# Forgetting attention with a spectral mix: a load moved ahead of a blocked one, mode products moved to mid-step, a small load moved to another queue

## The chip, the cores and the metric

The kernel runs on one core of a Trainium2 chip. The metric is the time of one execution on the device, in microseconds (us). The profile's span is some 1.7 to 2.0 us shorter than that time, so spans are compared with spans and times with times.

## The reference

There are two stages. The first is causal attention with a decay made from a forget gate f: for 8 batches and 8 heads, 576 positions, head width 64. The second takes the result x (8 x 576 x 512), keeps the 64 lowest frequencies of a real Fourier transform along the positions, multiplies each with its own complex 512 x 512 matrix, transforms back, and finishes with one more product.

```python
log_f = np.log(np.clip(f, 0.0001, 1.0)); cum = np.cumsum(log_f, axis=-1)
scores = scale * q @ k.T + cum[:, :, :, None] - cum[:, :, None, :]      # causal, softmax
x = attn @ v                                                           # (B, S, H*D)
X = np.fft.rfft(x, axis=1);  Xr, Xi = X.real[:, :64], X.imag[:, :64]
Yr = einsum('bmd,mde->bme', Xr, w_r) - einsum('bmd,mde->bme', Xi, w_i)
Yi = einsum('bmd,mde->bme', Xr, w_i) + einsum('bmd,mde->bme', Xi, w_r)
u = x + np.fft.irfft(Y, n=576, axis=1)
out = u + np.maximum(u @ w_ch, 0.0)
```

w_r and w_i are 64 x 512 x 512 in float32 each: together 134 MB, most of what the kernel reads.

## The kernel before

The kernel does both stages at once. There are 32 steps, one per head and pair of batches (and one more for the pipeline's end), and two steps share one *pair* of heads, whose q, k and v come in one load each. While these steps compute the attention, weight tiles of 2 x 512 KB (in bf16; the source is float32) stream in through a ring of 9 slots. `emit_modes(n)` multiplies with tile n and so frees its slot; `next_w()` issues the next tile, which needs a free slot. All loads that change the type come from one engine, POOL, and keep their program order. So a load that waits for a slot holds up every load behind it.

```python
NRING = 9                                  # weight tiles in the ring
STG = 3                                    # staged pairs of q, k, v

def pool_dma(dst, src):
    tc.keep_in_program_order(nc.gpsimd.dma_start(dst, src))

def emit_loads(pr):                        # k, q, v of one pair
    ...
        if nm == "v" and pr < 2:
            nc.sync.dma_start(dst, ap)     # the first two v: no cast, Sync queue
        else:
            pool_dma(dst, ap)
...
nc.sync.dma_start(ft[:], f.rearrange("b h s -> (b h) s"))
emit_loads(0)
... # log, cumulative sum, transposes, exp: the decay factors, then the Fourier basis
for s in range(NS + 1):                    # NS = 32 steps, B = 8, NTH = 32
    pr, h = s // 2, s % 2
    if h == 0 and pr + STG - 1 < NPR:
        emit_loads(pr + STG - 1)
    if s < 10 and nload < min(NRING, 3 + 3 * s // 4):
        next_w()                           # fill the ring
    if s == 10:
        pool_dma(wch[:], moe_w_ch.rearrange("(eb p) e -> p eb e", p=128))
    ... # transposes of the next pair, scores 0, first attention-value group, scores 1 and 2
    if s >= 1:
        emit_av(s - 1, [3, 4])             # second attention-value group
    ... # scores 3, v back, Fourier products of a finished pair
    if s > B:
        while nmode < (s - B) * NTH // (NS - B):
            emit_modes(nmode)              # first one: step 9; frees a ring slot
            nmode += 1
            next_w()                       # tenth tile: first one that needs a freed slot
```

The softmax here doesn't subtract the row's maximum and nothing guards it: scores larger than these inputs give would overflow.

## Time and profile before

| | before |
|---|---|
| time, median of the first 3 runs | 448.64 us |
| span of the profiled run | 446.5 us |
| bytes read from HBM | 163.73 MB |
| last weight landed | 405.3 us |
| rest (late products, output) | 41.2 us |

These are lines of the profile's page for the kernel before: the DMA rows of the 40-slice view (11.16 us a slice; first the mean busy share of the 16 DMA engines in tenths, then what they moved), the HBM total, and the chain of waits that ended last, by engine.

```profile
DMA  8999999999999999999999999999999999991698
GB/s 203 206 233 233 234 234 233 152 233 206 233 234 207 234 216 224 233 211 229 231 210 235 211 212 211 211 211 211 211 211 211 211 211 211 211 196 28 225 362 296
HBM read 163.73 MB, written 9.44 MB: 388 GB/s over the span
DMA 58%; PE 18%; DVE 7%; ACT 7%; issue 3%; POOL 1%; SPq 1%; DVEq 0%; ACTq 0%; POOLq 0%
```

From the first slice to 400 us the DMA engines are busy. The GB/s row counts what is written, in bf16 for most loads, so the reads behind 211 GB/s are about twice that. The one odd value is 152, in the eighth slice (78 to 89 us). A closer look, in windows of 1 us of the kernel before; the last two columns are the DMA share (1.2 is a full stream here) and GB/s:

```profile
core 0: us, PE busy (x) PEld busy (x) DVE busy (x) ACT busy (x) POOL busy (x), PEclk, DMA share, GB/s
78.00:79.00 1.00, 1.00 (x20) 0.83 (x21) 1.00 (x4) 0.64 (x3) 0.00 (x0) 1.00 1.24 207
79.00:80.00 1.00, 0.90 (x29) 0.88 (x30) 0.90 (x4) 0.99 (x2) 0.00 (x0) 1.00 0.78 129
80.00:81.00 1.00, 1.00 (x35) 0.97 (x31) 0.73 (x2) 0.04 (x1) 0.07 (x1) 1.00 0.28 51
81.00:82.00 1.00, 1.00 (x17) 0.65 (x15) 1.00 (x3) 1.00 (x2) 0.96 (x2) 1.00 0.11 27
82.00:83.00 1.00, 1.00 (x18) 0.76 (x17) 1.00 (x2) 1.00 (x2) 1.00 (x2) 1.00 0.63 48
83.00:84.00 1.00, 1.00 (x18) 0.55 (x18) 1.00 (x3) 0.77 (x2) 0.85 (x2) 1.00 1.18 179
```

For some 4 us the stream breaks. Who is late? This is the timeline of POOL, the issuer, at that time (start, duration, engine, line, what; in brackets the idle time before it and what ended it), and of the tensor engine's mode products (PE, L138):

```profile
64.76 0.74 POOL L88 DMA_DIRECT2D wb<-in_moe_w_i_dram  x1 [1.75 <-DMA wb<-in_moe_w_r_dram]
80.93 0.74 POOL L88 DMA_DIRECT2D wb<-in_moe_w_r_dram  x1 [15.43 <-PE tp L437]
...
82.43 0.71 POOL L88 DMA_DIRECT2D stk<-in_k_dram  x1
...
84.85 0.77 POOL L88 DMA_DIRECT2D wch<-in_moe_w_ch_dram  x1
```

```profile
77.70 0.17 PE L138 MATMUL A<-XT,wb 128*128 128x16 bf16 x1 [0.52 <-DVE XT L581]
79.70 0.92 PE L138 MATMUL A<-XT,wb 128*128 128x16 bf16 x31
```

The ninth tile was issued at 64.76 us. Then POOL stands still for 15.43 us, until the first mode product (32 matmuls, of which 31 run at 79.70 to 80.62) frees a slot. The profile names a neighbouring tensor-engine group as the releaser, but the tile it waits to overwrite is the one that L138 reads. Behind the blocked tile stand the next pair's k, q and v and w_ch, though none of them needs that slot. What had been issued before runs out at 79.4 us.

A load is spread over 16 DMA engines and counts as landed when all 16 have reported. The trace records each of the 16 reports. Here are those of the last loads around the hole (first and last report of each, worked out from the trace, in us):

```
                            first    last     spread
last load before the hole   79.42    81.45    2.03
first load after it         85.56    86.03    0.47
last weight of all          400.16   405.30   5.14
```

A 512 KB weight half takes 2.54 us at the stream's pace. So the first report lost 85.56 - 79.42 - 2.54 = 3.60 us in the hole, and the last one lost 86.03 - 81.45 - 2.54 = 2.04 us. I call these *first-engine loss* and *last-engine loss*, though the trace doesn't say which of the 16 engines a report comes from. The hole also pulls the spread together here, from 2.03 to 0.47 us: nearly all start even after it.

At the start, f is issued on Sync ahead of v. The timelines of Sync and Activation in the kernel before:

```profile
0.81 0.59 SPq L238 DMA_DIRECT2D Yacc<-in_f_dram  x1
1.46 1.07 SPq L217 DMA_DIRECT2D stv<-in_v_dram  x2
```

```profile
0.80 1.28 ACT L285 ACT_TABLE_LOAD   x1 [0.80 <-PEq L873]
3.66 0.68 ACT L285 ACTIVATE Yacc<-Yacc 64x576 f32<-64x576 f32 x1 [1.58 <-DMA Yacc<-in_f_dram]
```

f lands at 3.64 us, and the logarithm at 3.66 starts the chain that leads to the decay factors, and so to every step.

### The profile page before, as it was taken

How to read it: one execution, taken by the hardware profiler on the slowest of the kernel's cores; microseconds unless marked ns; L12 is line 12 of the kernel's file. 1: busy time of each engine (PE TensorE's matmuls, PEld its weight loads, DVE VectorE, ACT ScalarE, POOL GpSimd, SP SyncE). 2: the span in 40 equal slices, each digit the busy share in tenths (PEclk: the TensorE clock that was granted, in tenths of full speed). 3: DMA queues.
4: the chain of work that ended last, by engine and by line, in shares of the span. 5: the costliest groups of instructions: out<-in, count | busy, mean ns of one | idle time of the engine just before them, and what ended most of it. 6: DMA issues, size and time to landing. Idle time of an engine off the chain costs nothing.

```text
span 446.5 us, 11102 instructions
## 1 busy us (share of the span) xinstructions
PE 327.1 (73%) x4791; PEld 222.6 (50%) x4791; DVE 237.3 (53%) x602; ACT 202.4 (45%) x296; POOL 146.1 (33%) x194
## 2 busy tenths in 40 slices
PE   2388888989788788768597969999822238527993
PEld 1255555766566566556465746656612224323441
DVE  5768888776676546656377664223300002103894
ACT  3378888647567454664446533443200002102442
POOL 7333330534343323323333223232322323200661
PEclk9999999959599555897769578999955558856998
DMA  8999999999999999999999999999999999991698
GB/s 203 206 233 233 234 234 233 152 233 206 233 234 207 234 216 224 233 211 229 231 210 235 211 212 211 211 211 211 211 211 211 211 211 211 211 196 28 225 362 296
DMA packets 66431, 97.25 MB, mean 218 GB/s; under 512 B 3376, under 2 KB 44848, under 8 KB 66384
## 3 DMA queue, kind: packets, MB, share of 16 engines
q0 software_dynamic: 62480, 85.34, 103.3%
q1 hardware_dynamic: 3824, 11.09, 6.9%
q8 instruction: 37, 0.61, 0.5%
q10 hardware_dynamic: 80, 0.13, 0.1%
q14 instruction: 10, 0.08, 0.0%
HBM read 163.73 MB, written 9.44 MB: 388 GB/s over the span
## 4 chain that ended last, share of the span: by engine, by line
DMA 58%; PE 18%; DVE 7%; ACT 7%; issue 3%; POOL 1%; SPq 1%; DVEq 0%; ACTq 0%; POOLq 0%
DMA wb<-in_moe_w_i_dram 30%; DMA stk<-in_k_dram 13%; DMA stq<-in_q_dram 11%; ACT E L496 4%; DMA wb<-in_moe_w_r_dram 3%; PE tp L437 3%; PE pav L534 3%; PE pxw L680 3%; PE ps L489 3%; PE A L138 2%; DVE XT L581 2%; PE vp L461 1%; DVE uo L821 1%; PE ptr L669 1%; ACT KT L450 1%
## 5 line engine op out<-in xcount | busy, mean ns | idle before, releaser
L496 ACT ACTIVATE E<-ps 128x1024 bf16<-128x1024 f32 (+1 forms) x128 | 104.5, 859 | 39.3 <-PE ps L489 27.2
L138 PE MATMUL A<-XT,wb 128*128 128x16 bf16 x2048 | 71.6, 172 | 56.8 <-DMA wb<-in_moe_w_i_dram 35.0
L138 PEld LDWEIGHTS <-wb 128*128 128x128 bf16 x2048 | 64.0, 100 | 72.6 <-DMA wb<-in_moe_w_i_dram 38.2
L88 POOL DMA_DIRECT2D wb<-in_moe_w_r_dram x65 | 47.5, 731 | 134.7 <-PE A L138 30.4
L88 POOL DMA_DIRECT2D wb<-in_moe_w_i_dram x65 | 47.1, 725 | 78.2 <-DMA wb<-in_moe_w_i_dram 45.1
L489 PE MATMUL ps<-QTs,KT 64*128 64x64 bf16 (+4 forms) x384 | 57.5, 319 | 6.1 <-ACT E L496 5.9
L534 PE MATMUL pav<-va,E 128*128 128x65 bf16 (+1 forms) x1088 | 55.9, 210 | 4.3 <-DVE x_all L556 2.6
L534 PEld LDWEIGHTS <-E 128*128 128x128 bf16 (+1 forms) x1088 | 45.1, 114 | 15.8 <-issue 5.6
L153 DVE TENSOR_TENSOR YT<-A,Yacc 128x128 bf16<-128x128 f32 x24 | 8.9, 369 | 77.2 <-PE A L138 77.2
L511 DVE TENSOR_TENSOR E<-E,trimask 128x256 bf16<-128x256 bf16 (+2 forms) x128 | 38.2, 317 | 6.8 <-ACT E L496 6.4
L450 ACT COPY KT<-tp 128x640 bf16<-128x640 bf16 (+1 forms) x32 | 22.1, 745 | 26.6 <-PE tp L437 26.4
L687 ACT CAST XW<-pxw 128x512 bf16<-128x512 f32 x36 | 20.3, 587 | 29.8 <-PE pxw L680 25.1
L680 PE MATMUL pxw<-wch,yy 128*128 128x512 bf16 x144 | 33.5, 382 | 0.0
L699 ACT CAST yy<-pyw 128x512 bf16<-128x512 f32 x8 | 4.7, 586 | 60.7 <-PE pyw L692 60.7
L437 PE MATMUL tp<-ident_bf,kb 128*128 128x128 bf16 x144 | 16.1, 269 | 19.1 <-DVE kb L421 19.1
L556 DVE TENSOR_TENSOR x_all<-pav,rcp 128x384 bf16<-128x384 f32 x64 | 29.2, 456 | 0.9
L454 ACT COPY VT<-tp 128x640 bf16<-128x640 bf16 (+1 forms) x32 | 22.5, 753 | 12.6 <-PE tp L437 12.4
L489 PEld LDWEIGHTS <-KT 64*128 64x128 bf16 x384 | 18.1, 98 | 19.8 <-issue 11.6
L828 POOL TENSOR_TENSOR uo<-uo 128x1024 f32<-128x1024 f32 x7 | 16.5, 2359 | 29.3 <-DVE uo L821 25.5
L581 DVE CAST XT<-px 128x128 bf16<-128x128 f32 x32 | 21.0, 805 | 8.6 <-PE px L571 8.6
L425 DVE TENSOR_TENSOR vb<-stv,wdec 128x1152 bf16<-128x1152 f32 x16 | 21.6, 1351 | 5.4 <-PE tp L437 4.7
L452 DVE COPY QTs<-tp 128x640 bf16<-128x640 bf16 (+1 forms) x32 | 23.3, 767 | 0.8 <-PE tp L437 0.8
(108 smaller groups left out, 439.4 us busy)
## 6 DMA issues: line engine op xcount, KB each, us to landing
wb<-in_moe_w_r_dram POOLq DMA_DIRECT2D x63, 512.0 KB, 17.6
wb<-in_moe_w_i_dram POOLq DMA_DIRECT2D x63, 512.0 KB, 18.1
out_dram<-uo SPq DMA_DIRECT2D x16, 512.0 KB, 3.7
stv<-in_v_dram POOLq DMA_DIRECT2D x14, 576.0 KB, 15.6
stk<-in_k_dram POOLq DMA_DIRECT2D x16, 288.0 KB, 15.3
stq<-in_q_dram POOLq DMA_DIRECT2D x16, 288.0 KB, 15.3
stv<-in_v_dram SPq DMA_DIRECT2D x2, 576.0 KB, 6.1
out_dram<-uo SPq DMA_DIRECT2D x7, 128.0 KB, 3.9
```

Of the source, the lines that this page charges most:

```text
L88: tc.keep_in_program_order(nc.gpsimd.dma_start(dst, src))
L138: nc.tensor.matmul(A[:, eb, mi, :], lhsT=wb[:, t, mi, r * D + eb * 128 : r * D + (eb + 1) * 128], rhs=XT3[:, m, c0 : c0 + 2 * B], start=(i ...
L437: nc.tensor.transpose(tp[:, r - r0, :, :].rearrange("c h p -> c (h p)"), sb[:, r, :, :].rearrange("p b d -> p (b d)"), ident_bf[:, :],)
L450: nc.scalar.copy(rows(KTs[pr % 2][:, :, 0:S]), tv)
L452: nc.vector.tensor_copy(rows(QT[pr][:, :, :]), tv)
L489: nc.tensor.matmul(ps[:, b, o : o + n], lhsT=KTs[pr % 2][bs, h, jb * 128 : (jb + 1) * 128], rhs=QT[pr][bs, h, jb * 128 + c0 : jb * 128 + c ...
L496: nc.scalar.activation(E[:, :, piece * 512 : piece * 512 + w], ps[:, :, 0:w], ACT.Exp, scale=scale,)
L511: nc.vector.tensor_tensor(dg, dg, tr, ALU.mult)
L534: nc.tensor.matmul(pav[64 * half : 64 * half + w, slot, :], lhsT=E[:, b, c : c + (w - 1) * st + 1 : st], rhs=va[:, jb, b, :], start=(n == ...
L556: nc.vector.tensor_tensor(xo, pi, ri, ALU.mult)
L581: nc.vector.tensor_copy(_strided(XT3[:, 0, B + b : B + b + 1], [[3 * B, NM], [B, 2]]), px[:, :, :],)
L680: nc.tensor.matmul(pxw[:, :], lhsT=xT[:, eb, i * 128 : (i + 1) * 128], rhs=wch[:, eb, :], start=(eb == 0), stop=(eb == NDC - 1),)
```

## The change

Its intent is to keep the stream going where the tenth tile blocks: w_ch is issued in front of that tile, and the mode products, which free the slots, come earlier in a step. And f shall not stand in front of v on the Sync queue.

```diff
-        nc.sync.dma_start(ft[:], f.rearrange("b h s -> (b h) s"))
+        nc.scalar.dma_start(ft[:], f.rearrange("b h s -> (b h) s"))
...
-            if s == 10:
+            if s == 9:
                 pool_dma(wch[:], moe_w_ch.rearrange("(eb p) e -> p eb e", p=128))
...
                 emit_scores(s, 1)
                 emit_scores(s, 2)
+            if s > B:
+                while nmode < (s - B) * NTH // (NS - B):
+                    emit_modes(nmode)
+                    nmode += 1
+                    next_w()
             if s >= 1:
                 emit_av(s - 1, [3, 4])
...
-            if s > B:
-                while nmode < (s - B) * NTH // (NS - B):
-                    emit_modes(nmode)
-                    nmode += 1
-                    next_w()
```

## The prediction

> **What bounds the kernel.** DMA transfers. In the 40-slice view the DMA row is 9 from about 11 to 400 us except one slice. The chain of waits gives 58% of the span to DMA, 30% to the w_i tiles alone. HBM reads are 163.73 MB, which from 4 to 400 us is 413 GB/s, almost constant. Landings of equal 512 KB weight halves come every 2.5 us throughout. The last 41 us (405 to 446) are a tail: late mode products, output matmuls, output stores. Nothing in the change touches it.
>
> **The hole.** In half-microsecond windows the transfers are at 207 GB/s until 79.0 us, fall to 16-37 GB/s at 80.5-82.5, and are back at 83.5. The POOL timeline shows why: the ninth tile was issued at 64.76 us, then POOL waits 15.4 us for the first mode product, which frees a ring slot at about 80.6, and issues the tenth tile at 80.93. Pair 7's loads and w_ch stand behind it in the same program order. Only here, between the start and 400 us, does the stream break: the spread of the 16 engines' landing times grows steadily otherwise and collapses from 2.0 to 0.5 us only at this hole. From the landings, fast DMA engines lose about 3.6 us there and slow ones 2.0 us (time between landings less 2.54 us of transfer).
>
> **What the change does.**
> 1. w_ch (512 KB, 2.5 us of transfer) gets issued at about 66 us, ahead of the blocked tile. The backlog then ends at about 82 us instead of 79.4.
> 2. The first mode product moves ahead of the second attention-value group. Its operand XT is complete at 78.15 us, yet 31 of its 32 matmuls ran at 79.70-80.6, behind a transpose, a pav and a vp group. I expect it to end near 79.2, tile ten to be issued near 79.5, and its data to flow about 1.5-2 us later. Together 1 and 2 close the hole; either alone would close most of it.
> 3. f leaves Sync for the Activation queue, so v is issued about 0.6 us earlier (f's issue takes 0.59 us on Sync). The Trainium skill, "DMA: Bandwidth & Descriptors", section "Issuing engines are not separate DMA queues", says this saves only the issue time; I expect 0.2-0.5 us at the start, f itself landing up to 0.4 us later, since it shares with v. Activation's first table load shifts behind the issue, without harm.
>
> **How much counts.** After the hole everything is paced by the slowest DMA engine: the last weight's landings are spread over 5.1 us, and the tail waits for the last one. If the hole closes, the 2 us spread before it is carried on instead of being wiped out. So the gain is less than 3.6 us: about 1.7-2.6 us, plus about 0.3 from the start. No bytes, matmuls or copies go away.
>
> **Prediction.** 446.1 us, range 444.6 to 447.7. Faster by over 2%: 0.02; within 2%: 0.97; slower: 0.01.
>
> **Right if:** the 79-83 us windows hold about 207 GB/s; tile ten is issued at 79-80 us and w_ch before 70; the spread of landings at the end grows to 6-7 us; the last weight lands at about 402.5-403.5 us; tail length about 41 us as before. **Wrong if:** the hole only moves to the next mode products (around 88-96 us, where the tensor engine waits for pair 7's k); f's later landing delays the first steps and so the first slot; or the granted tensor clock, half at 388-409 us, stays half further into a tail that starts earlier, and eats 1 us or so of the gain.

## The result, and the profile after

The kernel after takes 446.95 us (median of 4 runs, 446.5 to 447.35) against 448.83 us for the kernel before (4 runs, 448.2 to 449.25). The ratio is 0.9961, with a 95% interval of 0.9947 to 0.9976: a gain of 0.4%, 1.9 us. That lies in the predicted range, 0.85 us above its centre.

The page of the kernel after (the HBM line reads the same 163.73 MB):

```profile
DMA  9999999999999999999999999999999999991698
GB/s 202 206 233 233 234 233 235 171 233 206 234 233 207 234 223 217 234 214 227 232 209 234 211 211 211 211 211 211 211 211 211 211 211 211 211 200 25 225 348 318
DMA 52%; PE 29%; DVE 7%; issue 3%; ACT 2%; POOL 1%; SPq 1%; DVEq 0%; ACTq 0%; POOLq 0%
```

The eighth slice has gone from 152 to 171 only. The windows of 1 us of the kernel after, as before:

```profile
80.00:81.00 1.00, 0.94 (x12) 0.62 (x12) 0.97 (x5) 0.64 (x4) 0.00 (x0) 1.00 1.24 206
81.00:82.00 1.00, 1.00 (x40) 0.99 (x37) 0.70 (x4) 1.00 (x2) 0.00 (x0) 1.00 1.18 197
82.00:83.00 1.00, 1.00 (x26) 0.86 (x22) 0.85 (x4) 0.35 (x1) 0.79 (x2) 1.00 0.63 115
83.00:84.00 1.00, 1.00 (x13) 0.53 (x11) 0.57 (x3) 0.84 (x2) 0.69 (x1) 1.00 0.40 53
84.00:85.00 1.00, 1.00 (x23) 0.91 (x23) 0.98 (x1) 1.00 (x2) 0.99 (x2) 1.00 1.03 128
```

The hole hasn't closed. It has moved from 79-83 us to 82-85 us and is shallower. POOL and the mode products of the kernel after show why:

```profile
67.08 0.74 POOL L88 DMA_DIRECT2D wch<-in_moe_w_ch_dram  x1 [1.77 <-DMA wb<-in_moe_w_i_dram]
82.21 0.74 POOL L88 DMA_DIRECT2D wb<-in_moe_w_r_dram  x1 [14.39 <-PE A L138]
```

```profile
80.06 0.17 PE L138 MATMUL A<-XT,wb 128*128 128x16 bf16 x1 [0.52 <-DMA wb<-in_moe_w_i_dram]
80.99 0.92 PE L138 MATMUL A<-XT,wb 128*128 128x16 bf16 x31
```

w_ch went out at 67.08, as meant, and lengthens the backlog by its 2.5 us. But the first mode product, though earlier within its step, ends at 81.91 us (80.99 + 0.92) instead of 80.62, and the tenth tile is issued 1.3 us *later* than before. Its whole step is about 2.3 us late (the single matmul that opens the group: 80.06 instead of 77.70). That lateness is there from the beginning. Activation and Sync in the kernel after:

```profile
0.80 0.56 ACTq L238 DMA_DIRECT2D Yacc<-in_f_dram  x1
1.39 1.28 ACT L285 ACT_TABLE_LOAD   x1 [1.39 <-PEq L873]
6.16 0.68 ACT L285 ACTIVATE Yacc<-Yacc 64x576 f32<-64x576 f32 x1 [3.48 <-DMA Yacc<-in_f_dram]
```

```profile
0.81 0.97 SPq L217 DMA_DIRECT2D stv<-in_v_dram  x2
```

f was issued at the same moment as before, 0.80 us, but lands at 6.14 us instead of 3.64. So one part of the change looks as if it fought the other two. That is a theory until it is tried.

### The profile page after: what moved, and what is told of

It reads as the page before. It is cut to its first block, busy times and chain, and to the rows that moved or that the text cites. A ratio compares the mean times of both kernels' runs of the same rounds, so it can differ in the third digit from the quotient of the medians.

```text
span 444.8 us, 11083 instructions
## 1 busy us (share of the span) xinstructions
PE 330.9 (74%) x4775; PEld 225.2 (51%) x4791; DVE 235.6 (53%) x602; ACT 202.1 (45%) x296; POOL 146.8 (33%) x194
## 3 DMA queue, kind: packets, MB, share of 16 engines
HBM read 163.73 MB, written 9.44 MB: 389 GB/s over the span
## 4 chain that ended last, share of the span: by engine, by line
DMA 52%; PE 29%; DVE 7%; issue 3%; ACT 2%; POOL 1%; SPq 1%; DVEq 0%; ACTq 0%; POOLq 0%
DMA wb<-in_moe_w_i_dram 24%; DMA stk<-in_k_dram 11%; DMA stq<-in_q_dram 8%; PE pxw L680 5%; PE ps L489 4%; PE pav L534 4%; PE tp L437 4%; PE A L138 4%; DMA stv<-in_v_dram 4%; DMA wb<-in_moe_w_r_dram 3%; PE px L571 2%; DVE XT L581 2%; PE ptr L669 1%; PE vp L461 1%; DVE uo L821 1%
## 5 line engine op out<-in xcount | busy, mean ns | idle before, releaser
L138 PE MATMUL A<-XT,wb 128*128 128x16 bf16 x2048 | 69.9, 172 | 48.9 <-DMA wb<-in_moe_w_i_dram 29.1
L489 PE MATMUL ps<-QTs,KT 64*128 64x64 bf16 (+4 forms) x384 | 63.3, 323 | 6.2 <-ACT E L496 6.1
L534 PEld LDWEIGHTS <-E 128*128 128x128 bf16 (+1 forms) x1088 | 46.6, 117 | 14.0 <-issue 6.6
L680 PE MATMUL pxw<-wch,yy 128*128 128x512 bf16 x136 | 32.6, 386 | 1.4 <-issue 1.0
L489 PEld LDWEIGHTS <-KT 64*128 64x128 bf16 x384 | 19.3, 98 | 22.7 <-issue 13.9
L545 DVE RECIPROCAL rcp<-pav 128x6 f32<-128x6 f32 x64 | 12.3, 192 | 24.9 <-PE pav L534 24.4
```

The costliest lines, as they stand in the source:

```text
L138: nc.tensor.matmul(A[:, eb, mi, :], lhsT=wb[:, t, mi, r * D + eb * 128 : r * D + (eb + 1) * 128], rhs=XT3[:, m, c0 : c0 + 2 * B], start=(i ...
L489: nc.tensor.matmul(ps[:, b, o : o + n], lhsT=KTs[pr % 2][bs, h, jb * 128 : (jb + 1) * 128], rhs=QT[pr][bs, h, jb * 128 + c0 : jb * 128 + c ...
L534: nc.tensor.matmul(pav[64 * half : 64 * half + w, slot, :], lhsT=E[:, b, c : c + (w - 1) * st + 1 : st], rhs=va[:, jb, b, :], start=(n == ...
L680: nc.tensor.matmul(pxw[:, :], lhsT=xT[:, eb, i * 128 : (i + 1) * 128], rhs=wch[:, eb, :], start=(eb == 0), stop=(eb == NDC - 1),)
```

## The experiments

Theory A: f's late landing delays the whole chain by 2.3 us, and that keeps the hole open; with f on Sync the other two parts would close it. The rival B: f's move is a small gain, as predicted, and the hole depends on something else. Rival C: the mid-step mode products do most of the work. The losses and landings in this table are worked out from the trace of each run's profiled execution, as explained above; "mid" and "end" say where the mode products stand in a step. The last report is what the end waits for: in each of these profiled runs the span ends 40.7 to 42.1 us after it.

| run | f on | w_ch in step | modes | median us | ratio to before, 95% | first-engine loss | last-engine loss | last weight: first, last report |
|---|---|---|---|---|---|---|---|---|
| before | Sync | 10 | end | 448.83 | 1 | 3.60 | 2.04 | 400.16, 405.30 |
| after | Activation | 9 | mid | 446.95 | 0.9961 (0.9947 to 0.9976) | 2.23 | 1.22 | 398.90, 404.07 |
| e1_f_sync | Sync | 9 | mid | 446.20 | 0.9950 (0.9936 to 0.9963) | 0.52 | 0.69 | 396.84, 402.64 |
| e2_f_only | Activation | 10 | end | 451.23 | 1.0060 (1.0048 to 1.0073) | 6.03 | 4.72 | 402.74, 408.16 |
| e3_wch_only | Sync | 9 | end | 447.70 | 0.9980 (0.9967 to 0.9992) | 1.31, then 0.69 | 0.52, then 1.41 | 398.46, 405.14 |
| e4_modes_only | Sync | 10 | mid | 447.71 | 0.9983 (0.9971 to 0.9996) | 2.70 | 1.77 | 399.13, 404.56 |
| after_again | Activation | 9 | mid | 446.78 | 0.9962 (0.9950 to 0.9974) | 2.13 | 2.40 | 398.51, 403.77 |
| e1_again | Sync | 9 | mid | 446.33 | 0.9948 (0.9936 to 0.9960) | 0.31 | 0.01 | 396.92, 403.71 |
| e7_f_sync_loads7 | Sync | 9, and pair 7 | mid | 445.53 | 0.9934 (0.9921 to 0.9947) | no hole | no hole | 396.44, 403.14 |
| e8_f_act_loads7 | Activation | 9, and pair 7 | mid | 445.97 | 0.9939 (0.9927 to 0.9951) | no hole | no hole | 396.61, 402.54 |
| e7_again | Sync | 9, and pair 7 | mid | 446.23 | 0.9948 (0.9935 to 0.9960) | no hole | no hole | 396.43, 403.24 |

### f back on Sync: e1_f_sync

```diff
 (the kernel after)
-        nc.scalar.dma_start(ft[:], f.rearrange("b h s -> (b h) s"))
+        nc.sync.dma_start(ft[:], f.rearrange("b h s -> (b h) s"))
```

> The kernel after, with f put back on Sync ahead of v (w_ch early and mid-step modes kept). Theory A: in the kernel after, f landed at 6.1 us instead of 3.6, which made the whole first chain, and so the first mode product, 2.3 us later and kept the hole open. Then here f lands at about 3.6 us, the first mode product ends at about 79.4 us instead of 81.8, the stream never breaks near 79-85 us, and the time is about 445.5 us (faster than after by 1.2 or so). Theory B (f beside v starts the stream earlier and is worth its 0.3 us or more; the hole is set by something else, such as the step order): the hole stays at 2 us or more for the fast engines and the time is 447.2 or above.

f lands at 3.52 us, and the same 1 us windows in this run hold the stream nearly full:

```profile
80.00:81.00 1.00, 1.00 (x26) 0.85 (x25) 0.85 (x4) 0.29 (x1) 0.85 (x2) 1.00 1.25 207
81.00:82.00 1.00, 1.00 (x12) 0.57 (x12) 0.55 (x3) 0.91 (x2) 0.68 (x2) 1.00 1.19 198
82.00:83.00 1.00, 1.00 (x23) 0.89 (x22) 1.00 (x1) 1.00 (x2) 1.00 (x2) 1.00 1.21 183
```

The first mode product ends at 79.85 us (expected 79.4) and the tenth tile is issued at 80.15. The first-engine loss is down to 0.52 us. The time, 446.2 us, is below that of the kernel after but not as far as expected (445.5); whether it differs at all is taken up again below.

### f's move alone: e2_f_only

```diff
 (the kernel before)
-        nc.sync.dma_start(ft[:], f.rearrange("b h s -> (b h) s"))
+        nc.scalar.dma_start(ft[:], f.rearrange("b h s -> (b h) s"))
```

> The kernel before, with only f moved to the Activation queue. Theory A: f lands 2.5 us later, the first mode product ends at about 83 us, the hole grows by about 2.3 us for all DMA engines, the time is about 450.5 us. Theory B (f's move is a gain or harmless): 448.5 us or less, hole as in before.

451.23 us: f's move by itself costs 2.7 us. The hole grows for the first engine from 3.60 to 6.03 us, by 2.43, about what the chain is late (the tenth tile is issued at 83.47 us, 2.54 later). Theory A holds, and B is out: at the start nothing is won that reaches the hole, whose last load before it first reports at 79.56 us against 79.42.

### w_ch alone: e3_wch_only

```diff
 (the kernel before)
-            if s == 10:
+            if s == 9:
```

> The kernel before, with only w_ch moved from step 10 to step 9. Backlog ends 2.5 us later (about 82 us) while the tenth tile is issued at about 80.9 as before: the hole shrinks from 3.6 us (fast engines) and 2.0 us (slow) to under 1 us and 0. Theory A: about 446.0 us, so w_ch alone gives nearly all that the three parts give together, or more. Rival C (the mid-step modes do the work): 448 us or more.

447.70 us, not 446.0: a third of the gain that was expected. The old hole did shrink, from 3.60 to 1.31 us, not to under 1. But a second one opened at 97 to 100 us, where the DMA share falls to 0.94 (a full stream shows 1.2). POOL's timeline in this run, with the eleventh and the twelfth tile:

```profile
85.54 0.76 POOL L88 DMA_DIRECT2D wb<-in_moe_w_r_dram  x1 [0.63 <-PE A L138]
...
96.22 0.74 POOL L88 DMA_DIRECT2D wb<-in_moe_w_r_dram  x1 [9.18 <-PE A L138]
```

The twelfth tile goes out at 96.22, too late: the last load before it reports first at 97.61, and data flow in full only some 2 us after an issue (the kernel before issues its tenth tile at 80.93 us, and the stream is full again at 83). In the kernel before, that load reported first at 100.17 and the twelfth tile went out at 95.27. Both ends of the margin moved. The loads in front of the twelfth tile are the same in both kernels, but behind the shorter first hole the stream gets through them 2.56 us sooner. And the tile is issued 0.95 us later, since the computing that frees its slot waits for pair 7's k. The first report of k comes at the same time as before (89.70 against 89.67), for it now stands behind w_ch, but behind the shorter hole its reports are further apart (1.24 against 0.33 us). Here is that wait in the chain of waits, in the kernel before and, below it, in this run (start and duration; k lands at 90.00 and at 90.94 us):

```profile
82.43 7.57 DMA stk<-in_k_dram
82.77 8.18 DMA stk<-in_k_dram
```

This is the case that the prediction named under "Wrong if", a hole that moves to the next mode products; it came with w_ch alone. In e1_f_sync, with the mode products in mid-step, the twelfth tile goes out at 87.93 (also from POOL's timeline), and there is no second hole. So the two parts need each other.

### Mid-step modes alone: e4_modes_only

```diff
 (the kernel before)
                 emit_scores(s, 2)
+            (the while loop with emit_modes and next_w)
             if s >= 1:
                 emit_av(s - 1, [3, 4])
...
-            (the while loop with emit_modes and next_w)
```

> The kernel before, with only the mode products moved to mid-step. Theory A: the first mode product ends at about 79.4 us instead of 80.6 and the tenth tile is issued about 1.2 us earlier, so the hole shrinks by 1.2 us to 2.4 (fast) and 0.8 (slow): about 447.7 us. Rival C (the mid-step modes do most of the work, by freeing ring slots earlier in every step): 446.8 us or less.

447.71 us, as theory A expected. The tenth tile is issued at 79.92 us, 1.0 us earlier than before, and the hole shrinks by 0.9 us. Rival C is out.

The first four runs together: the single parts measured -0.8 (w_ch), -0.8 (modes) and +2.7 us (f) in medians against 448.5 for the kernel before in these rounds. Their sum is +1.1. All three together measured -1.9. The parts don't add. In first-engine loss they are -1.6 (w_ch, both holes), -0.9 and +2.4, together -0.1, and all three measured -1.4; 0.7 of the difference is the second hole, which w_ch alone opens and the mid-step modes prevent. Where the rest comes from isn't shown.

### Why f is late: e5_f_alone_on_act and e6_swapped

Is the Activation queue slow to start, or does f wait behind v?

```diff
 e5 (the kernel after)
-                if nm == "v" and pr < 2:
+                if nm == "v" and pr < 0:      # all v on POOL, nothing beside f
 e6 (e1_f_sync: f on Sync)
-                    nc.sync.dma_start(dst, ap)
+                    nc.scalar.dma_start(dst, ap)   # the first two v on Activation
```

> The kernel after, with the first two v loads moved from Sync to the POOL queue, so that f on the Activation queue has no v beside it (POOL's own transfers start their packets only at 4.5 us and later). Theory P (f waits because v's two loads, issued at the same moment on Sync, are served first): f's first packet at about 2.2 us, f lands at about 3.6 us. Theory Q (a load from the Activation queue starts late by itself): f's first packet at about 3.8 us as in the kernel after, f lands at 5 us or later. No statement on the total time: v itself comes later.

> The two queues swapped: f on Sync, both v loads on the Activation queue (w_ch early, mid-step modes). Theory Q: v's first packet at about 3.8 us, f's at 2.2, f lands at 3.6. Theory P: no such delay of the Activation queue as such: either v's packets start near 2 us and f's only near 3.8, or f's come first at about 2 us and v's follow right behind, at 2.5-2.8 us.

Activation's timeline in e5 and, below it, in e6:

```profile
0.80 0.56 ACTq L238 DMA_DIRECT2D Yacc<-in_f_dram  x1
1.39 1.28 ACT L285 ACT_TABLE_LOAD   x1 [1.39 <-PEq L873]
3.49 0.68 ACT L285 ACTIVATE Yacc<-Yacc 64x576 f32<-64x576 f32 x1 [0.81 <-DMA Yacc<-in_f_dram]
```

```profile
0.81 0.95 ACTq L217 DMA_DIRECT2D stv<-in_v_dram  x2
1.79 1.28 ACT L285 ACT_TABLE_LOAD   x1 [1.79 <-PEq L873]
5.87 0.68 ACT L285 ACTIVATE Yacc<-Yacc 64x576 f32<-64x576 f32 x1 [2.79 <-DMA Yacc<-in_f_dram]
```

Alone on Activation, f lands at 3.46 us: that queue isn't slow (theory P, against Q). With the queues swapped, f is on Sync, where it was fast before, and lands late all the same, at 5.84 us. So it's neither queue but the two loads being issued at the same moment. The packets in the trace (2,304 bytes each; a v load has 256, f has 64) tell the order:

```
run           v's first packet   f's first packet   v packets begun before f's first   v packets after f's last
after         1.90               3.78               214 of 512                         212
e2_f_only     1.90               3.85               208                                201
e6_swapped    1.88               3.82               224                                222
after_again   1.91               3.88               215                                218
```

f comes in between the two v loads: when its first packet starts, 208 to 224 of the 256 packets of the first v load have started (199 in e8_f_act_loads7, which comes below). The Trainium skill has a reason for it, on the page "DMA: Bandwidth & Descriptors", section "Queues, rings and completion order": each DMA engine takes turns between the queues it has work for, but drains a whole packet of some 9 to 17 descriptors from one before it switches (I take what the page calls a descriptor for what the trace counts as a packet). A v load has 256 / 16 = 16 of them per engine, f has 4. So "taking turns" would mean here: all of the first v load, then f, then the second v. The counts agree with that; the switching on one engine can't be seen, since the trace doesn't name the engine of a packet. A rival would give the same counts and wasn't tried: that the packets of one load after the other, v, f, v, are made ready in the order of issue whatever the queue. That f starts only when most of a v load has started is shown; which of the two makes it wait is not. Why v is first at equal issue times isn't shown either; its first packet starts at 1.9 us, f's starts at 2.15 when it is alone (e5).

### Does the late chain cost anything but the hole? after_again, e1_again, e7_f_sync_loads7, e8_f_act_loads7

The loads of pair 7 don't need the blocked slot either. Issued in front of the tenth tile, they add 4.3 us of backlog (three loads at 1.4 us), enough for either chain. The staging buffer that they fill was last read in step 7, so nothing else has to change.

```diff
 e7 (e1_f_sync) and e8 (the kernel after)
-            if h == 0 and pr + STG - 1 < NPR:
+            if h == 0 and s != 10 and pr + STG - 1 < NPR:
                 emit_loads(pr + STG - 1)
...
             if s == 9:
+                emit_loads(7)
                 pool_dma(wch[:], ...)
```

> The kernel after, unchanged, on the same chip and in the same rounds as the next three. 446.9 us, about 1.9 us under the kernel before; hole of about 2.2 us (fast engines).

> The kernel after with f back on Sync, again. Theory A: 0.7 to 1.5 us faster than the kernel after of the same rounds. Theory B: not faster.

> f on Sync, w_ch early, mid-step modes, and pair 7's k, q and v also issued at step 9 ahead of the tenth tile: 4.3 us more of backlog in front of the blocked tile. The hole of 0.5 us that was left in f-on-Sync closes entirely; first engine's last weight landing at about 396.3 us. Gain over f-on-Sync at most 0.6 us, perhaps none, as the slowest engine decides: 445.6 to 446.3 us.

> The kernel after (f on the Activation queue, landing at about 6 us, first mode product at about 81.8 us), with pair 7's loads issued at step 9 ahead of the tenth tile. Theory A (f's late landing costs time only through the hole): with 4.3 us more of backlog the hole is gone though the compute chain is still 2.3 us late, and the time equals that of the run before this one within 0.5 us. Rival D (the late chain costs time otherwise too): at least 1 us slower than it.

There is no hole in e7 and none in e8, though in e8 f still lands at 6.21 us. The means of these rounds are 445.66 (e7) and 445.82 us (e8), 0.15 apart with an uncertainty of about 0.9, so theory A stands: where the backlog covers the block, a chain that is 2.3 us late costs nothing that these runs can see. Against after_again (mean 446.92) e8 is 1.1 us faster and e7 1.25 us. For e7 445.6 to 446.3 us was expected; 445.53 is 0.07 below that.

Is f on Sync (e1) faster than the kernel after? In these rounds 446.31 against 446.92 us on average, 0.61 apart, a little less than the expected 0.7 to 1.5, and not clear by itself. With the runs of all three jobs, 10 and 9, the difference is 0.72 us, with a 95% interval of about 0.26 to 1.18. The jobs ran on more than one chip, so this is rough: taken against the kernel before in the same rounds, the first runs differ by 0.53 us and the repeats by 0.61. So f's move, which costs 2.7 us alone, costs some 0.6 us inside the change. The best versions found are e7 and e8, 0.5 to 0.7% under the kernel before; between e1 and e7 no difference is clear: a repeat of e7 gave 446.23.

### Where the rest of the hole goes: e7_again and e9_more_fetches

In e7 the first-engine loss of 3.60 us is gone entirely, and the first report of the last weight is 3.7 us earlier (396.44 against 400.16). But its last report is only 2.2 us earlier, in the profiled run. The spread among the 16 engines has grown from 5.14 to 6.70 us. The prediction said so: a hole wipes the spread out, and without it the spread is carried on. What makes an engine slow? A candidate is instruction fetch: the trace has 37 packets of 16 KB on the instruction queue. Each takes 0.9 to 1.0 us of one engine, and the spread grows along with them:

```
                        before                              e7_again (no hole)
load reporting at   fetch packets so far   spread      fetch packets so far   spread
33 us               0                      0.88        0                      1.46
48                  2                      2.02        2                      2.59
80                  5                      2.03        5                      2.60
100                 7                      1.57        8                      2.37
200                 19                     2.71        18                     4.58
300                 28                     4.00        29                     5.67
396                 35                     5.14        35                     6.77
```

To get more of them, the next run adds some 2,230 instructions that do nothing to engines which are mostly idle in the streaming stage.

```diff
 (e7_f_sync_loads7, in the loop over the last 31 tiles)
             while nmode < last - 1:
+                for i in range(40):
+                    nc.vector.memset(jd[0:1, 0:1], 0.0)
+                    if i % 5 < 4:
+                        tc.keep_in_program_order(nc.gpsimd.memset(jp[0:1, 0:1], 0.0))
                 emit_modes(nmode)
```

> Control for the next run: f on Sync, w_ch early, mid-step modes, pair 7's loads early. 445.5 us; 37 instruction-fetch packets of 16 KB; the last weight's landings spread over about 6 us among the 16 DMA engines.

> The same kernel with some 1,240 one-element memsets added on the vector engine and 990 on POOL, spread over the weight-streaming stage in which both are mostly idle; the data and the results stay the same. Theory S (each 16 KB instruction fetch holds one DMA engine for about 1 us, which nothing gives back where the stream never breaks; so the spread of landings, and the time, is the count of fetches on the unluckiest engine): about 9 more fetch packets, the spread grows by 1 to 2 us and the time with it, to 446.5-447.5 us. Rival N (the spread has another cause, and instructions on idle engines are free): spread and time as in the control within 0.4 us.

The control came out at 446.23 us (445.5 expected), with 37 packets and a spread of 6.81 us (about 6). The experiment itself failed: 505.2 us. The timelines of POOL and, in the last line, of the vector engine (DVE) in e9 show why:

```profile
299.41 0.72 POOL L88 DMA_DIRECT2D wb<-in_moe_w_i_dram  x1
300.12 4.63 POOL L716 MEMSET jp<- 1x1 f32 x32
305.15 0.71 POOL L88 DMA_DIRECT2D wb<-in_moe_w_r_dram  x1 [0.40 <-issue]
465.07 37.70 DVE L714 MEMSET jd<- 1x1 f32 x333
```

The 32 memsets take 4.63 us on POOL, the engine that issues every tile, so a tile now takes about 6.45 us (305.15 less 298.70, the issue before) instead of 5.1, and the last weight comes 21.4 us later than in the control (424.65 against 403.24). The larger part is at the very end: 333 of the vector engine's memsets were left over and run for 37.7 us after its last useful work. Nor did the run add what it was meant to: the 16 KB packets are still 37, and it is the 8 KB packets of another instruction queue that went from 10 to 28. So the 16 KB packets don't follow the vector engine's and POOL's instructions. They may be the tensor engine's; this is an estimate: 18 more packets of 8 KB for some 2,230 instructions are 124 instructions each, so 248 in 16 KB, and the tensor engine's 9,594 records in the trace of the kernel before would fill 39 of these.

So no run has changed the number of 16 KB packets. But the traces at hand say more than the table. Add up, for one weight load, how much later than the first each of its other 15 reports comes. In the eleven runs of the experiments' first table, for loads from 108 to 392 us, this sum changes from one load to the next by -0.03 us on average where no instruction packet lies between them (191 cases, standard deviation 0.23), and grows by 1.10 us across exactly one 16 KB packet (134 cases, 0.22). So the spread grows at these packets, each about once its own length, and not between them. In e7_again the sum grows by 41.8 us from 32 to 395 us, and the 46 instruction packets of that time (36 of 16 KB, 10 of 8 KB) took 37.1 us. That is a match in time, case by case, and not yet a run that changed the packets.

## Why the prediction was right or wrong

The centre was 446.1 us, the measured median is 446.95, inside the range of 444.6 to 447.7. The direction and the class were right. Yet there is luck in it: the range, 3.1 us wide, is wider than the whole gain, and of the prediction's six signs of being right the kernel after shows two (w_ch before 70 us, the tail). The other four failed: the stream broke (115 GB/s at 82 to 83 us), tile ten went out at 82.21 us, the last spread was 5.17 us, and the last weight landed at 404.07. In the prediction's own sum, 1.7 to 2.6 us for the hole fits what e1 gained on the kernel before in the same rounds, 2.3 to 2.4 us on average; the 0.3 us for f was about -0.6. Point by point:

- *What bounds the kernel, the hole, its cause and its size.* Right. In every run of the table the first-engine loss tells when the last weight first reports, within some 0.3 us: before to e1, 3.1 us less loss and 3.3 us earlier; before to e2, 2.4 us more and 2.6 us later.
- *w_ch at about 66 us, backlog to about 82.* Right: 67.08, and the last load before the hole first reports at 82.11 in the kernel after.
- *"f itself landing up to 0.4 us later", 0.2 to 0.5 us of gain at the start.* This is the step that failed. f landed 2.5 us later (6.14 against 3.64) and cost about 2.7 us alone and some 0.6 us inside the change. The prediction leaned on the Trainium skill, "DMA: Bandwidth & Descriptors", section "Issuing engines are not separate DMA queues", that issuing from another engine saves only the issue time, and put f's sharing with v at 0.4 us at most, without working out how long f could stand behind v. Here f stood behind nearly a whole v load: 214 of its 256 packets had begun before f's first. The list of what might go wrong did name this case.
- *The first mode product to end near 79.2, tile ten near 79.5.* Wrong for the kernel after (81.91 and 82.21), because of f. Without f's move, 79.85 and 80.15 (e1): moving to mid-step gave 0.8 us, not 1.4, since the transposes of v still run ahead of it and the whole group opened 0.3 us later (77.99 instead of 77.70).
- *"Either alone would close most of it."* Wrong. Mid-step modes alone closed 0.9 of 3.6 us. w_ch alone closed 2.3 us and opened a second hole of 0.7 (first engine) to 1.4 us (last engine), so 1.6 us net.
- *The gain is less than the hole, since the spread is carried on.* Right where the hole is closed: the spread at the end is 5.8 to 6.8 us in e1, e7 and e8, with 6 to 7 predicted. In the kernel after the hole stayed, the spread collapsed again (from 1.65 to 0.64 us) and ended at 5.17. A hole doesn't always do this: in after_again, with a hole of 2.13 us, fifteen reports came within 0.30 us of each other and one 1.88 us late.
- *Last weight at 402.5 to 403.5, tail about 41 us.* 404.07 in the kernel after, 402.64 in e1. The tail was 40.72 us, no longer than before (41.2), so the harm that the prediction feared from the granted clock didn't show.

## What to carry to other kernels

In a stream that is bound by transfers, look for the one place where the issuer blocks, and put in front of it every load that does not need what it waits for; then check the next block too: the stream reaches it sooner, and a load that the computing waits for may now land later. A change that makes a small load wait for its turn behind a big one can undo this from the other end of the kernel: what the first chain of a pipeline waits for goes first, alone, on whichever queue. And parts of a change that act on the same hole are not to be added up: try each one alone and leave each one out.

## What the Trainium skill lacked or had wrong

- "DMA: Bandwidth & Descriptors", "Issuing engines are not separate DMA queues": it says that issuing from several engines only saves issue time. Here it changed the order too: f, issued at 0.80 us beside a v load, landed at 6.14 us, and at 3.46 us without one. A word that a small load can stand behind most of a 590 KB load from another issuer would have helped.
- The same page doesn't say which of two loads issued at the same moment from Sync and Activation is first. Here it was v in all five traces where they met, on either queue (v's first packet at 1.9 us, f's at 3.8 to 3.9).
- "Runtime: NRT & Kernel Launch", "Instruction fetch mechanics": it calls the cost of crossing a 16 KiB boundary mostly hidden. Here each such fetch packet takes 0.9 to 1.0 us of one DMA engine, 37 in a run, and in a stream without holes the spread of the engines' reports grows from 1.46 to 6.77 us. The lateness summed over a load's reports grows by 1.10 us across one such packet and by -0.03 us without (134 and 191 cases). No run changed the number of these packets (the one that was to failed).
- The same section has the blocks at 16 KiB for all engines. In the run with 2,230 more vector and POOL instructions the 16 KB packets stayed at 37 and packets of 8 KB went from 10 to 28.
- No page has it that the 16 engines' reports of one load drift apart in a long stream, and that a break in the stream mostly pulls them together again (2.03 to 0.47 us in the kernel before, but 1.61 to 1.88 us in after_again, where one report stayed late).
